# Four of the twelve token-weight tiles turned by DMA transposes instead of TensorE, with the first half of the step list rearranged

## The chip, the cores and the metric

One core of one Trainium2 chip runs one kernel launch. The metric is device time in microseconds of that launch. The kernel before was run three times: 165.80 us is the median, 165.77 and 166.24 us are the ends. Its inputs and its output are in the chip's memory; five engines take part: TensorE (PE; its weight loads are listed apart, as PEld), VectorE (DVE), ScalarE (ACT), GpSimd (POOL) and SyncE (SP), which only issues transfers. ACT also issues transfers from its own queue, and POOL some from a third.

## What is computed

A recurrent attention with a decay for each head feeds a block that mixes tokens and channels. Batch is 4, heads 8, tokens 768, head width 64, so the model width is 512.

```python
for t in range(S):
    state = gamma * state + outer(k[:, :, t], v[:, :, t])
    y[:, :, t] = scale * q[:, :, t] @ state
x = y with heads side by side                       # (4, 768, 512)
theta = x @ w_theta
zr, zi = x * cos(theta), x * sin(theta)
y = w_tok_r @ zr + w_tok_i @ zi                     # over tokens, for each batch
u = x + y
out = u + relu(u @ w_ch)
```

## The kernel before

The recurrence is computed in chunks. A unit `n` (0 to 23) is one batch, one chunk of 256 tokens and half of the heads: batch `n // 6`, chunk `n // 2 % 3`, half `n % 2`. A tile `C` or `t` (0 to 23) is 128 tokens of one batch, all 512 columns; units 0 and 1 make tiles 0 and 1, units 2 and 3 make tiles 2 and 3, and so on. The third number in a step such as `M.3.1` is a token tile of the same batch.

The order of all work is written out by hand as one list of steps, `ORDER`. Each step `name.args` calls the function of that name, which issues its instructions at once; a trailing letter picks the engine (`v` DVE, `a` ACT, `p` POOL) or, for loads and stores, the queue (`s` SP, `a` ACT). Each engine and each queue runs its own instructions strictly in the order of the list, and semaphores make an instruction wait for its data. So the list sets, for each engine, what stands behind a waiting instruction.

The steps, in the order in which a unit and then a tile go through them:

- `Lk`, `Lq`, `Lv` load 256 KB of k, q or v. The tiles are `kqf` (16 buffers for k and q together) and `vf` (9).
- `ck`, `cq` cast k and q to bf16; `cqs` (line 342) casts q and scales it by a decay in one pass; `cv` (line 348) scales v. Results are `kqb` and `vb`.
- `Tk`, `Tq` (line 356) turn k and q with four 128x128 transposes each on TensorE, into `kq_ps`; `E` copies that to `kqT`. `Dk` (line 372) does both with one DMA transpose on SP's queue.
- `A` (line 390) makes the scores in the one buffer `at_ps`; `m` (line 399) multiplies them by the causal mask on DVE; `I` (line 455) and `Y` (line 467) add what the state and the chunk give to the output; `ST` (line 417), `S0`, `S1`, `SB` carry the state on.
- `XB` copies the unit's output to `xT`, where q was scaled by `cqs`; `XA` (line 485, DVE only) copies and scales it, where q was only cast by `cq`.
- `Tx` (line 499) and `Ex` turn `xT` to `x_sb` by TensorE and a copy; `Dx` (line 506) does it with one DMA transpose on SP.
- `Hh` (line 513) makes theta; `CN` (line 520) takes sine and cosine on ACT; `z` (line 527) multiplies by x, on DVE or POOL.
- `Pw.r.g` loads a group of rows of token weight `r` (0 real, 1 imaginary) on POOL's queue, with a cast to bf16: group 0 is row tile 0, group 1 tiles 1 and 2, group 2 tiles 3 to 5. `Pth` and `Pch` load the two channel weights.
- `Tw.r.t` (line 535) turns row tile `t` of weight `r` with six 128x128 transposes on TensorE into `w_ps`, and `Ew` copies it to its place in `wtr` or `wti`.
- `M.t.s` (line 553) adds two matmuls, weights 0 and 1, of source tile `s` to the output tile `t`; it needs the turned weights of row tile `t % 6` and `z` of source tile `s`. The first batch's tile 3 needs `Tw.0.3` and `Tw.1.3`, its tile 5 needs `Tw.0.5` and `Tw.1.5`.
- `u`, then `Tu` and `Eu`, or `Du` (line 575) by a DMA transpose on SP, then `O` (line 580), `f` and the store `SO` finish a tile.
- `Z` runs two matmuls on zeros: filler for TensorE, with no result that is used.

The constants are steps too. `const3` computes two tables of decays with Exp on ACT (line 274), `const8` and `const9` the rest of them; `const7` runs Sin once on one number (line 285), `const6` zeroes the block-diagonal state tiles (line 306).

Of the kernel before, what the change touches and what calls it, by code (L numbers as in the profile page):

```python
# [677 lines left out]
```

## Time and profile before

| | before |
|---|---|
| median of three runs | 165.80 us |
| the profiled execution, its own time | 165.54 us |
| its span, first to last instruction | 163.8 us |
| TensorE clock granted over the span | 1.000 |
| DMA transposes issued by SP | 37 (16 `uT`, 12 `x_sb`, 9 `kqT`) |
| bytes read from memory, written to it | 25.69 MB, 6.29 MB |
| 16 DMA engines' share: SP's and ACT's queues, POOL's queue | 67.6% + 15.2%, 12.4% |

The profile is of one execution. Its span leaves 1.7 us of the measured time outside. A row of a group or timeline gives line, engine, operation, output <- inputs, shapes and a count; "idle before" is the time that the engine stood still ahead of these instructions, with the releaser that ended it. Rows of an engine's name with a q (SPq, ACTq) are issues on its queue. Matmul ends are modelled, so what one of a row of matmuls costs is best read from how far apart they start.

### The profile page before, as it was taken

Reading aid. Unit: us, or ns where it says so; the run is one execution under the profiler, and the core shown is the slowest. Engines: PE = TensorE matmul, PEld = TensorE weight load, DVE = VectorE, ACT = ScalarE, POOL = GpSimd, SP = SyncE. Lnnn points to the kernel's source line nnn. Section 1 sums busy time; section 2 is a strip of 40 time slices with the busy share of each in tenths; the row PEclk is TensorE's granted clock in tenths of the full one; section 3 lists DMA queues with packets and bytes.
Section 4 is the critical chain, followed back from the end, with each engine's and each line's share of the span. In section 5 each row is a group of like instructions: output and inputs, shape, how many; then the busy total and the mean of one; then the engine's idle time right before and its main releaser. Section 6 shows DMA issues by size and latency. Waiting matters only on the chain.

```text
span 163.8 us, 4900 instructions
## 1 busy us (share of the span) xinstructions
PE 153.7 (94%) x2001; PEld 87.1 (53%) x2030; DVE 115.2 (70%) x218; ACT 79.5 (49%) x142; POOL 77.3 (47%) x111
## 2 busy tenths in 40 slices
PE   5997889999999999999999999999999999999992
PEld 1355655756666655654555565554554544444550
DVE  5488687987994897994779894798867760244462
...
GB/s 130 318 317 255 279 310 233 268 230 214 207 193 202 308 220 198 309 135 259 341 270 198 192 229 189 223 151 292 218 267 116 96 92 202 160 70 123 71 243 203
DMA packets 62918, 34.93 MB, mean 213 GB/s; under 512 B 26416, under 2 KB 59952, under 8 KB 62896
## 3 DMA queue, kind: packets, MB, share of 16 engines
q1 hardware_dynamic: 51680, 23.73, 67.6%
q10 hardware_dynamic: 8528, 7.47, 15.2%
q0 software_dynamic: 2688, 3.41, 12.4%
q8 instruction: 16, 0.26, 0.7%
...
HBM read 25.69 MB, written 6.29 MB: 195 GB/s over the span
## 4 chain that ended last, share of the span: by engine, by line
PE 84%; DVE 5%; POOL 4%; issue 3%; ACT 1%; DVEq 0%; POOLq 0%
PE y_ps L553 36%; PE o_ps L580 12%; PE th_ps L513 12%; PE r_ps L467 5%; PE at_ps L390 4%; PE kq_ps L356 3%; PE r_ps L455 3%; PE w_ps L535 3%; DVE at L399 2%; PE x_ps L499 2%; PE y_ps L605 2%; PE r_ps L417 2%; PE u_ps L565 1%; DVE kqT L140 1%; POOL mask L298 1%
## 5 line engine op out<-in xcount | busy, mean ns | idle before, releaser
L553 PE MATMUL y_ps<-z,wti 128*128 128x512 bf16 x131 | 49.6, 379 | 1.0 <-issue 1.0
L553 PE MATMUL y_ps<-z,wtr 128*128 128x512 bf16 x131 | 49.7, 379 | 0.3
L527 POOL TENSOR_TENSOR z<-cs,x_sb 128x1024 bf16<-128x1024 bf16 x12 | 25.3, 2122 | 17.4 <-DMA x_sb<-xT 9.8
L399 DVE TENSOR_TENSOR at<-at_ps,mask 128x1024 bf16<-128x1024 f32 x24 | 29.2, 1216 | 0.6 <-PE at_ps L390 0.5
L348 POOL TENSOR_TENSOR vb<-vf,vsc 128x512 bf16<-128x512 f32 x17 | 18.2, 1071 | 21.3 <-DMA vf<-in_v_dram 20.3
L586 DVE SCALAR_TENSOR_TENSOR ot<-o_ps,u 128x512 f32<-128x512 f32 x23 | 15.8, 688 | 12.8 <-PE o_ps L580 12.7
L513 PE MATMUL th_ps<-wth,xT 128*128 128x512 bf16 x88 | 23.9, 379 | 0.5
L560 DVE TENSOR_TENSOR u<-y_ps,x_sb 128x512 bf16<-128x512 f32 x23 | 15.8, 688 | 11.9 <-PE y_ps L553 11.8
L580 PE MATMUL o_ps<-wch,uT 128*128 128x512 bf16 x88 | 23.2, 379 | 0.4 <-issue 0.2
L520 ACT ACTIVATE cs<-th_ps,zerob 128x512 bf16<-128x512 f32 x24 | 16.4, 685 | 12.6 <-PE th_ps L513 8.1
L520 ACT ACTIVATE cs<-th_ps,halfpi 128x512 bf16<-128x512 f32 x24 | 16.3, 684 | 10.8 <-issue 4.6
L140 POOL CAST sbd<-s 64x256 bf16<-64x256 f32 (+1 forms) x21 | 10.0, 478 | 22.9 <-DVE s L435 21.7
L553 PEld LDWEIGHTS <-wtr 128*128 128x128 bf16 x138 | 13.5, 98 | 12.7
L553 PEld LDWEIGHTS <-wti 128*128 128x128 bf16 x138 | 13.5, 98 | 11.9 <-DVE wti L140 0.2
L138 ACT COPY kqT<-kq_ps 128x1024 bf16<-128x1024 bf16 x12 | 12.1, 1012 | 10.4 <-PE kq_ps L356 10.4
L138 ACT CAST kqb<-kqf 128x512 bf16<-128x512 f32 x17 | 10.2, 619 | 6.8 <-DMA kqf<-in_k_dram 6.7
L513 PEld LDWEIGHTS <-xT 128*128 128x128 bf16 x96 | 8.8, 98 | 8.2
L580 PEld LDWEIGHTS <-uT 128*128 128x128 bf16 x92 | 8.4, 98 | 8.6
L356 PE MATMUL kq_ps<-ident,kqb 128*128 128x128 bf16 x120 | 11.2, 219 | 0.5 <-ACT kqb L138 0.2
L311 PE MATMUL zz<-zero 128*128 128x512 bf16 x27 | 9.7, 494 | 2.0 <-DVE part L232 1.9
L467 PE MATMUL r_ps<-at,vb 64*64 64x128 bf16 x384 | 9.9, 221 | 1.0 <-DVE at L399 1.0
L356 PEld LDWEIGHTS <-kqb 128*128 128x128 bf16 x120 | 8.1, 98 | 4.7 <-ACT kqb L138 0.7
...
## 6 DMA issues: line engine op xcount, KB each, us to landing
vf<-in_v_dram SPq DMA_DIRECT2D x20, 256.0 KB, 5.7
kqf<-in_k_dram SPq DMA_DIRECT2D x19, 256.0 KB, 5.0
kqf<-in_q_dram SPq DMA_DIRECT2D x17, 256.0 KB, 5.3
out_dram<-ot ACTq DMA_DIRECT2D x12, 256.0 KB, 2.8
out_dram<-ot SPq DMA_DIRECT2D x11, 256.0 KB, 3.1
kqf<-in_q_dram ACTq DMA_DIRECT2D x7, 256.0 KB, 5.3
kqf<-in_k_dram ACTq DMA_DIRECT2D x5, 256.0 KB, 5.2
vf<-in_v_dram ACTq DMA_DIRECT2D x4, 256.0 KB, 5.3
```

The lines of the kernel that those rows point to most:

```text
L138: nc.scalar.copy(dst, src)
L348: engines[e].tensor_mul(in_blocks(vb), by_token(raw["vf", n]), _bcast_last(K["vsc"][:, i, :, h * HU:(h + 1) * HU], D))
L356: nc.tensor.transpose(st["kq_ps", n][:, 4 * w + x, :], st["kqb", n][:, w, x * P:(x + 1) * P], K["ident"])
L399: nc.vector.tensor_mul(at.rearrange("p g j a t -> p (g j) (a t)"), st["at_ps", n].rearrange("p g j a t -> p (g j) (a t)"), _bcast_mid(K["m ...
L467: nc.tensor.matmul(st["R", n + 1][c][g * D:(g + 1) * D, j * P:(j + 1) * P], st["vb", n][rows, lo:lo + D], st["at", n][rows, g, j, a, :], s ...
L513: nc.tensor.matmul(th_ps, st["xT", C][:, j, :], K["wth"][:, j, :], start=(j == 0), stop=(j == 3))
L520: nc.scalar.activation(st["cs", C][:, w, :], st["th_ps", C], AF.Sin, bias=K["zerob" if w else "halfpi"], scale=1.0)
L527: engines[e].tensor_mul(st["z", b][:, c], st["cs", C], _bcast_mid(x_of(C), 2))
L553: nc.tensor.matmul(st["y", t], K["wT"][r][:, s0, t0 * P:(t0 + 1) * P], st["z", b][:, s0, r, :], start=(done == 0 and r == 0), stop=(done = ...
L560: nc.vector.tensor_add(st["u", t], st["y", t], st["x", b][:, t0, :])
L580: nc.tensor.matmul(o_ps, st["uT", t][:, j, :], K["wch"][:, j, :], start=(j == 0), stop=(j == nD - 1))
L586: nc.vector.scalar_tensor_tensor(st["ot", t], st["o", t], 0.0, st["u", t], ALU.max, ALU.add)
```

## The change

`Dw` is new: one DMA transpose on SP's queue takes a bf16 row tile (128x768) to its place in `wtr` or `wti`. Row tiles 3 and 5 of both weights go that way; their four `Tw` and four `Ew` are gone. Unit 15's k and q go by `Dk` instead of `Tk`, `Tq` and `E`; tile 5's u by `Du` instead of `Tu` and `Eu`; tiles 8 and 12 go from `Tx` and `Ex` to `Dx`, tile 13 the other way. In all, TensorE issues 40 transposes fewer: 24 of weights, 8 for unit 15, 4 for tile 5's u and 4 for x.

`const3` is split: the Exp of `vsc` stays in it, that of `qsc` is the new step `constS`. `const7`, the Sin on one number, moves ahead of both. Loads move between SP and ACT; several casts and copies change engine; which units scale q early (`cqs`, then `XB`) and which late (`cq`, then `XA`) changes. The last 296 of the steps are the same.

```diff
ORDER = """
-const2 Lv.0.s const1 constQ const6.v Z.29 Z.2 const5 Z.38 Lk.0.a const3 Z.35 Z.8 Lq.0.s Lv.1.s Z.28 constA
-const4 Lq.1.a cqs.0.v const9 Lk.1.s cv.0.p Z.39 const8 ck.0.p Tk.0 Tq.0 ck.1.a E.0.v Lq.4.a ST.0
-Lk.4.a Z.15 A.0 cqs.1.p Tq.1 Lq.2.s S0.0.v SB.0.1.v Lk.2.s SB.0.0.p cv.1.p Lv.2.s S1.0 I.0 Z.27 m.0
-Tk.1 E.1.a Y.0 ST.1 XB.0.1.a cqs.2.v Z.34 S0.1.v S1.1 cv.2.p SB.1.0.a Pth Lq.3.s Z.18 XB.0.0.v Tq.2
-A.1 SB.1.1.a ck.2.a Tk.2 const7 I.1 Z.23 m.1 Y.1 XB.1.0.a Lk.3.s E.2.v XB.1.1.v A.2 ck.3.p m.2 ST.2
-S0.2.v S1.2 SB.2.1.a Z.11 cqs.3.p Tq.3 Lv.3.s Tx.0 Tk.3 Z.3 ck.4.p Lv.4.s Lk.5.s Lq.5.s Lv.5.s
-Lq.6.s Lk.6.s Lv.6.s Lq.7.s E.3.a SB.2.0.v I.2 Y.2 XB.2.1.a Ex.0.a cv.3.v cq.4.p Tk.4 Lq.8.s A.3
-ST.3 Lk.7.s S0.3.v SB.3.0.a S1.3 Lv.7.s Lk.8.s Tx.1 Tq.4 SB.3.1.p cv.4.p m.3 Pw.1.0 XB.2.0.a Ex.1.a
-I.3 Lv.8.s E.4.a cq.5.a Y.3 Pw.0.0 ST.4 Hh.0 ck.5.a S0.4.v XB.3.0.v XB.3.1.v cv.5.v CN.0.1 A.4
-CN.0.0 Tq.5 Hh.1 Tk.5 SB.4.0.p SB.4.1.a Pw.0.1 Hh.2 m.4 E.5.v I.4 Y.4 ST.5 ck.6.a Tk.6 Tx.2 cq.6.a
-CN.1.1 CN.1.0 XA.4.1 A.5 XA.4.0 m.5 Lq.9.s Ex.2.v S0.5.v z.0.p Tq.6 E.6.a CN.2.0 cv.6.p Hh.3
-SB.5.0.v Tx.3 Tw.1.0 z.1.v SB.5.1.a Ew.1.0.v Ex.3.a CN.2.1 A.6 I.5 Y.5 ST.6 XA.5.0 z.2.v Tw.0.0
-CN.3.0 Tx.4 CN.3.1 Ew.0.0.v S0.6.v XA.5.1 Ex.4.v Hh.4 CN.4.0 CN.4.1 Tw.0.1 M.0.1 Pw.1.1 z.3.v M.0.0
-Tw.0.2 Pw.1.2 Ew.0.2.a SB.6.1.a Hh.5 z.4.p SB.6.0.p Lk.9.a M.0.3 ck.7.p cqs.7.p M.0.2 CN.5.1 CN.5.0
-cq.8.a m.6 Ew.0.1.v Tw.1.1 Tw.1.2 Ew.1.1.v Lv.9.s M.0.4 M.1.0 Tx.5 Ew.1.2.v M.1.1 S1.6 Tk.7 M.1.4
-Pch Ex.5.v z.5.v cv.7.v Tq.8 Tq.7 M.1.2 E.7.a M.0.5 I.6 Y.6 ST.7 A.7 ck.8.a u.0 S0.7.v m.7 XA.6.1
-SB.7.1.a M.1.5 M.1.3 XA.6.0 Tw.1.3 M.2.5 Pw.0.2 M.2.3 u.1 S1.7 Tk.8 M.2.1 M.2.0 SB.7.0.v Ew.1.3.a
-Tu.0 I.7 cv.8.p E.8.a cv.9.p Y.7 ST.8 A.8 cqs.9.v ck.9.v M.2.4 Du.1 Lk.10.s Eu.0.a XB.7.1.a XB.7.0.v
-S0.8.v SB.8.0.v M.2.2 Tx.6 Tq.9 Tk.9 Lv.10.a cv.10.p ck.10.p Lq.10.s S1.8 u.2 m.8 O.0 E.9.a SB.8.1.a
-Hh.6 Tw.1.4 I.8 Y.8 A.9 CN.6.0 Du.2 Lq.14.s CN.6.1 Ex.6.v f.0 ST.9 Tw.0.3 Hh.7 Ew.1.4.v Ew.0.3.a
-S0.9.v Tw.0.4 M.3.0 Tw.1.5 CN.7.0 CN.7.1 M.3.2 Dx.7 M.3.1 M.3.5 M.3.3 Lv.12.s Lk.12.s Ew.1.5.v
-XA.8.1 Ew.0.4.v Lq.12.s M.3.4 u.3 S1.9 Tw.0.5 Tk.10 M.4.5 cqs.10.p XA.8.0 m.9 M.4.3 Tq.10 SB.9.1.a
-SB.9.0.a I.9 O.2 Lq.11.s Lk.11.s E.10.a Lk.15.s Ew.0.5.v Lk.14.s Y.9 ST.10 A.10 z.7.p Lv.11.s
-XB.9.1.a XB.9.0.a f.2 M.4.0 O.1 M.4.1 cqs.14.p m.10 S0.10.v f.1 cq.11.a ck.12.v M.4.4 M.4.2 Tu.3
-Eu.3.a Dx.9 SB.10.0.a cqs.12.p u.4 Hh.9 Tq.11 ck.11.v Tu.4 z.6.v Eu.4.v ck.15.v M.5.0 M.5.4 Tk.11
...
+const2 Lv.0.s const1 constQ Z.8 const7 Lq.0.s Lk.0.s constA const3 Z.2 Z.35 Z.11 const4 Lv.1.a constS Z.38
+Z.27 Lk.3.s const5 cqs.0.v cv.0.v ck.0.v Lq.1.s Tk.0 Lk.2.a Tq.0 const9 ck.3.v cqs.1.v ST.0 Tq.1 Z.28 Z.29
+S0.0.v E.0.v Lk.1.s A.0 Lq.4.a ck.1.p cv.1.p const8 const6.v Tk.3 Lq.2.a SB.0.1.a Lv.2.s SB.0.0.a Tk.1 S1.0
+m.0 I.0 Pth Lv.3.s Z.39 Lk.4.s Y.0 E.1.a ck.2.v cq.2.p ST.1 Z.15 A.1 S0.1.v Tq.2 SB.1.1.a Tk.2 cv.3.p Z.3
+Lq.3.s cv.2.p cq.3.p SB.1.0.a XB.0.0.v cq.4.p XB.0.1.v S1.1 m.1 I.1 E.2.a Lv.4.s Y.1 ST.2 A.2 S0.2.v
+SB.2.1.p XB.1.0.v Z.34 S1.2 Tq.3 SB.2.0.a XB.1.1.a m.2 Lq.5.s Z.23 Lk.6.a Tx.0 Ex.0.v cv.4.p Lk.5.s I.2 Y.2
+Lv.5.s ST.3 E.3.a S0.3.v ck.4.a cqs.5.p A.3 Tk.4 SB.3.0.a XA.2.1 Lv.7.a Pw.1.0 Tq.4 Pw.0.0 Pw.0.1 SB.3.1.v
+Z.18 XA.2.0 E.4.a Hh.0 ck.5.a S1.3 I.3 Lq.6.s CN.0.1 Tx.1 m.3 Y.3 ST.4 A.4 XA.3.0 Pw.1.1 Ex.1.a CN.0.0 Tk.5
+Tq.5 E.5.a Lv.6.s S0.4.v Tx.2 m.4 SB.4.0.a Hh.1 CN.1.0 Lv.8.s cv.5.p XA.3.1 A.5 CN.1.1 SB.4.1.p I.4 cqs.6.p
+Y.4 ST.5 z.0.v S0.5.v ck.6.v Ex.2.a Hh.2 Tk.6 XA.4.1 SB.5.0.p Tq.6 CN.2.0 z.1.v XA.4.0 Hh.3 E.6.a SB.5.1.p
+m.5 Lq.8.a I.5 cv.6.p Tw.1.0 Ew.1.0.v Tx.3 Y.5 ST.6 CN.2.1 A.6 Ex.3.v XB.5.0.v CN.3.1 Tw.0.0 z.2.p Hh.4
+Lq.7.s Ew.0.0.v Lk.8.s Tx.4 XB.5.1.a Tw.0.1 CN.3.0 S0.6.v Ex.4.v CN.4.0 S1.6 M.0.2 Ew.0.1.v Pw.1.2 Tx.5
+M.0.0 Lk.7.s CN.4.1 Pw.0.2 Tw.0.2 Hh.5 SB.6.1.v z.3.v Ew.0.2.a cv.7.v z.4.v Lq.9.s CN.5.1 M.0.1 ck.7.p
+SB.6.0.p Tw.1.1 M.0.3 CN.5.0 Ew.1.1.v M.0.4 M.1.3 M.1.4 Ex.5.a cv.8.v z.5.v M.1.0 M.1.2 cq.7.a Tk.7 Tq.7
+Lk.9.s m.6 Tw.1.2 Lv.9.s M.0.5 M.1.1 Dw.1.3 E.7.v I.6 cqs.9.v Y.6 u.0 ST.7 A.7 ck.8.a Ew.1.2.a Tk.8 XB.6.1.v
+S0.7.v SB.7.0.v M.2.5 m.7 SB.7.1.v cqs.8.p Tq.8 XB.6.0.a M.2.4 S1.7 Tu.0 M.2.2 M.2.1 E.8.v Pch I.7 Eu.0.v
+M.1.5 cv.9.p Y.7 ST.8 S0.8.v XA.7.1 ck.9.a Lq.11.s A.8 Dw.0.3 Tk.9 Tw.1.4 XA.7.0 u.1 Lq.10.s Ew.1.4.a Du.1
+M.2.3 S1.8 Tq.9 SB.8.1.p M.2.0 SB.8.0.a Hh.6 Dw.0.5 u.2 I.8 m.8 Tx.6 O.0 E.9.a CN.6.1 Lk.10.a CN.6.0 Y.8
+ST.9 S0.9.v f.0 cqs.10.p A.9 Tw.0.4 Du.2 SB.9.0.a XB.8.1.v Hh.7 Ex.6.a cqs.11.p M.3.1 Ew.0.4.a Lv.10.a
+Lk.11.a M.3.3 SB.9.1.p M.3.2 M.3.0 M.3.4 CN.7.0 M.3.5 m.9 cv.10.p Tq.10 Dx.7 Dw.1.5 CN.7.1 M.4.0 Lq.12.a
+ck.10.v M.4.1 M.4.4 u.3 M.4.2 XB.8.0.v Lk.14.s z.6.v S1.9 z.7.p O.2 Tk.10 ck.11.p Lv.11.s M.4.3 M.4.5 I.9
+Lk.12.s f.2 O.1 E.10.a cv.11.p Lq.15.a u.4 Y.9 ST.10 f.1 A.10 Tq.11 XB.9.1.a M.5.1 M.5.5 M.5.2 Lv.12.a Tk.11
+S0.10.v m.10 M.5.4 Lq.14.s SB.10.1.p Hh.9 Tu.3 ck.12.p ck.14.a E.11.v cqs.12.p SO.2.s M.5.3 Dx.9 Lq.13.a
...
@@ -267,12 +262,14 @@
     def const3():
         K["qsc"] = const.tile([P, 2, nI * 4, 2], FT, name="qsc")
         K["vsc"] = const.tile([P, nI, 2, H], FT, name="vsc")
-        for t, arg, bias, sc in (
-                (K["qsc"].rearrange("p h x g -> p (h x) g"),
-                 K["argq"].rearrange("p h x g -> p (h x) g"), K["lscale"], 1.0),
-                (K["vsc"].rearrange("p i a h -> p (i a) h"), K["arg"], K["zerob"], -1.0)):
-            nc.scalar.activation(t, arg, AF.Exp, bias=bias, scale=sc)
+        nc.scalar.activation(K["vsc"].rearrange("p i a h -> p (i a) h"), K["arg"], AF.Exp,
+                             bias=K["zerob"], scale=-1.0)
         K["qx"] = const.tile([P, H // 2, S], FT, name="qx")
+
+    def constS():
+        nc.scalar.activation(K["qsc"].rearrange("p h x g -> p (h x) g"),
+                             K["argq"].rearrange("p h x g -> p (h x) g"), AF.Exp,
+                             bias=K["lscale"], scale=1.0)
 
     def const8():
         decay(0, 2 * P)
@@ -534,6 +531,11 @@
         for s0 in range(nT):
             nc.tensor.transpose(w_ps[:, s0, :], row[:, s0 * P:(s0 + 1) * P], K["ident"])
         st["w_ps", r, t0] = w_ps
+
+    def Dw(r, t0):
+        g = sum(t0 >= hi for _, hi in groups)
+        nc.sync.dma_start_transpose(out=K["wT"][r][:, :, t0 * P:(t0 + 1) * P],
+                                    in_=K["row"][r][g][:, t0 - groups[g][0]])
 
     def Ew(r, t0, e):
         copy(e, K["wT"][r][:, :, t0 * P:(t0 + 1) * P], st["w_ps", r, t0])
```

73 lines of the change are left out of this document (35 added, 38 removed).

## The prediction

> **What bounds the kernel now.** I read the page's head first, then the sums by stage (busy us of each engine, the granted clock, the DMA share, GB/s), then the chain of waits and the timelines of the first 56 us.
>
> ```profile
> span 163.8 us, 4900 instructions
> PE 153.7 (94%) x2001; PEld 87.1 (53%) x2030; DVE 115.2 (70%) x218; ACT 79.5 (49%) x142; POOL 77.3 (47%) x111
> 0.00:8.00 8.00, 6.00 (x19) 2.22 (x20) 4.18 (x15) 4.63 (x8) 6.33 (x36) 1.00 0.76 221
> 8.00:16.00 8.00, 6.91 (x164) 4.40 (x164) 6.70 (x13) 6.84 (x14) 7.17 (x9) 1.00 1.15 291
> 16.00:24.00 8.00, 6.58 (x141) 4.57 (x142) 5.84 (x13) 6.42 (x12) 3.78 (x7) 1.00 1.14 293
> 24.00:32.00 8.00, 7.65 (x153) 5.13 (x153) 6.71 (x14) 7.33 (x13) 4.59 (x4) 1.00 1.14 254
> 64.00:72.00 8.00, 7.81 (x144) 4.88 (x144) 6.75 (x13) 5.28 (x10) 4.44 (x4) 1.00 0.91 262
> 152.00:164.00 12.00, 8.55 (x52) 4.58 (x51) 5.20 (x9) 1.33 (x3) 0.00 (x0) 1.00 0.60 174
> ```
>
> TensorE is busy 153.7 of 163.8 us, so it stands still 10.1 us. The first four stages hold 32 - 27.14 = 4.9 us of that (and the zero matmuls as filler), the last one about 3.3 us of its span. That leaves under 2 us for the 120 us between: from the fourth stage to the tail TensorE sets the time, and what is taken off its queue there comes off the end, as long as nothing it needs gets later. In the first 32 us chains of other engines set it.
>
> **The 40 transposes taken away.**
>
> ```profile
> 33.46 0.34 PE w_ps L535 x6
> 35.52 0.67 PE w_ps L535 x12
> 38.37 0.45 PE kq_ps L356 x8
> ```
>
> These are pieces of the chain of waits. Twelve transposes follow each other in 0.67 us, eight in 0.45: 0.056 us each. The diff takes away 24 + 8 + 4 + 4 = 40: **-2.24 us**, all at places after 41 us where TensorE is the bound. The copies that fall away with them (Ew, E, Eu, Ex) free DVE and ACT, which are at 70% and 49%; I give nothing for that.
>
> **The start.** The rearranged steps make some things later, and I follow unit 0 and then unit 5.
>
> ```profile
> 2.73 0.51 SPq L164 DMA_DIRECT2D kqf<-in_k_dram  x1
> 4.90 0.61 SPq L160 DMA_DIRECT2D kqf<-in_q_dram  x1
> SPq L160 <- DMA kqf<-in_k_dram: 1.6, 1, 1.6
> kqf<-in_q_dram SPq DMA_DIRECT2D x17, 256.0 KB, 5.3
> 3.28 1.09 DVE L306 MEMSET sbd<- 128x256 uint32 x4
> 8.40 0.69 DVE L140 COPY kqT<-kq_ps 128x1024 bf16<-128x1024 bf16 x1 [1.18 <-PE kq_ps L356]
> 9.88 1.21 DVE L399 TENSOR_TENSOR at<-at_ps,mask 128x1024 bf16<-128x1024 f32 x1
> 11.02 0.68 DVE L342 TENSOR_TENSOR kqb<-kqf,qsc 128x512 bf16<-128x512 f32 x1
> ```
>
> In the list before, the fifth load on SP (Lq.2, at 4.90) waited 1.6 us until a k load had landed that ACT had issued. It is the ninth of both queues together, and no data ties it to that load: I read a ring of eight completion slots that SP's and ACT's transfers share in the order of the list. In the new list Lq.1 is SP's fifth but the sixth of both, so it need not wait: it goes out some 0.6 us after the fourth at 2.73, near 3.3, and lands 5.3 us later at about 8.6. DVE now has E.0 behind ck.3 and cqs.1: cqs.1 (0.68) ends near 9.3, E.0 (0.69) near 10.0, then const6 (1.09), which has moved here, and S1.0 (0.28, an estimate from such adds); m.0 starts near 11.3 where it started at 9.88. Unit 0 is 1.4 us late.
>
> ```profile
> 27.20 1.22 DVE L399 TENSOR_TENSOR at<-at_ps,mask 128x1024 bf16<-128x1024 f32 x1
> 29.30 0.35 PE at_ps L390 x16
> 29.92 0.42 PE L467 MATMUL r_ps<-at,vb 64*64 64x128 bf16 x16
> 12.80 0.62 ACT L138 CAST kqb<-kqf 128x512 bf16<-128x512 f32 x1
> 13.44 1.28 ACT L285 ACT_TABLE_LOAD   x1
> 14.73 0.29 ACT L285 ACTIVATE one<-zerob,halfpi 128x1 f32<-128x1 f32 x1
> ```
>
> Before, m.5 ended at 28.42 and Y.5 began at 29.92: 1.5 us of slack, since TensorE had other work queued ahead. That absorbs the 1.4. But const7 was what loaded ACT's Sin table at 13.44, in a gap. In the new list it runs first, Exp (const3, constS, const9, const8) puts another table in its place, and the first CN has to load Sin again: a third load, 1.28 us, between ck.5 and CN.0.1, with E.5 three steps behind it. A.5 waits for E.5, and in the new list I.4 and Y.4 stand behind A.5 on TensorE. So Y.5 is between on time (the load falls into ACT's slack) and 1.4 + 1.28 - 1.5 = 1.2 us late. Besides, A.6 (0.35) stood ahead of Y.5 and now stands behind it, so an equal Y.5 is a loss of 0.35. Cost of the start: 0.35 to 1.55; a gain is not excluded for units 2 to 4, whose loads come earlier, and I let the bottom end be -0.5. I take **+0.5**, near the end where the slack covers, since ACT is 6.42 of 8 us busy there and has 20% to give.
>
> [...]
>
> **The four DMA transposes, on SP's queue.**
>
> ```profile
> 27.37 1.52 POOL L187 DMA_DIRECT2D row<-in_moe_w_tok_i_dram  x2
> row<-in_moe_w_tok_i_dram POOLq DMA_DIRECT2D x1, 576.0 KB, 11.9
> row<-in_moe_w_tok_r_dram POOLq DMA_DIRECT2D x1, 576.0 KB, 8.9
> 30.89 0.69 DVE L527 TENSOR_TENSOR z<-cs,x_sb 128x1024 bf16<-128x1024 bf16 x1
> L527 POOL TENSOR_TENSOR z<-cs,x_sb 128x1024 bf16<-128x1024 bf16 x12 | 25.3, 2122 | 17.4 <-DMA x_sb<-xT 9.8
> L372 SPq DMA_TRANSPOSE kqT<-kqb x9: 1231/1252/2490, 60.0 to 122.3; - x9
> uT<-u SPq DMA_TRANSPOSE x16, 3.4
> kqT<-kqb SPq DMA_TRANSPOSE x9, 4.6
> 45.46 0.63 SPq L160 DMA_DIRECT2D kqf<-in_q_dram  x1
> 50.94 1.04 POOL L342 TENSOR_TENSOR kqb<-kqf,qsc 128x512 bf16<-128x512 f32 x1
> 55.23 0.39 PE L356 MATMUL kq_ps<-ident,kqb 128*128 128x128 bf16 x4
> 51.82 2.16 PE y_ps L553 x10
> ```
>
> No transpose of a weight by DMA is in this trace; a Dw moves 192 KB, between a Du (128 KB, lands in 3.4 us) and a Dk (256 KB, 4.6), and keeps SP 1.2 to 2.5 us, as the Dks do. I take 1.25 and a landing after 4.0.
>
> What comes late is the rows. Pw.1.2, the second of the pair at 27.37, now stands on POOL behind z.2, which DVE ran at 30.89 and POOL now runs in 2.12 us from about 29.7 (an estimate: CN.2 ends a little earlier in the new list). It goes out near 31.8 and lands 11.9 later, near 44; Pw.0.2 right behind it lands 8.9 to 11.9 after 32.6, near 44 too. So SP sits at Dw.1.3 until 44, then issues Dw.1.3 (to 45.3), Lq.11 (to 45.9), Dw.0.3 (to 47.2) and Lq.10 at 47.2 where it stood at 45.46. Behind these wait Du.1, Dw.0.5, Du.2, Dx.7, Dw.1.5 and the loads of units 11 to 14.
>
> Two things are due. M.3 (the row of 51.82 is M.3 and what follows) now begins with M.3.1: three Tw and two M (3 x 0.34 + 2 x 0.43) are no longer ahead of it, so it is due near 50.0 + 0.5; Dw.0.3 lands at 47.2 + 4 = 51.2. And Tq.10, which started near 55.0 in the row of 55.23, is due near 55.0 - 4 x 0.34 - 0.22 - 2 x 0.43 + 0.5 = 53.1 (four Tw, Tk.10 and two M fewer ahead); Lq.10 lands at 47.2 + 5.3 = 52.5, cqs.10 takes 1.04, ready at 53.5. TensorE stands 0.7 us for the first, and the second is then covered by it. The ends: 0, if the rows land 8.9 us after their issue as the real weight's did, and 4 us, if each Dw keeps SP 2.5 us and lands after 5.5. I take **+0.7**, with the median issue of nine Dks rather than the longest.
>
> ```profile
> q1 hardware_dynamic: 1633, 0.39, 38.8%
> x_sb<-xT SPq DMA_TRANSPOSE x2, 2.4
> DMA  9999999996299999999999006999999999999999
> ```
>
> **The DMA engines.** The first two rows are of the stretch from 127 to 132 us, where three 128 KB transposes (0.39 MB) are nearly all that moves: 38.8% of 5 us is 1.94, 0.65 us of all 16 engines each. The change adds four of 192 KB, one of 256 KB and two of 128 KB (Dx 12 and 8 for 13 make one, Du.5 the other): 4 x 0.97 + 1.3 + 1.3 = 6.5 us of all engines, four fifths of it between 44 and 80 us. The third row is DMA in 40 slices from 42 to 60 us: full, but for three slices of 0.45 us. From 64 to 72 us the share is 0.91 where the stages from 8 to 24 us reach 1.15 (records overlap, so a share can pass 1): 0.24 x 8 = 1.9 us of room, and 1.3 in the idle slices. These 3.2 us hide half of it; the other half I cost at nothing as well, on the guess that the loads that it delays are not the next ones due. With that cover gone it is 3.3 us.
>
> **Sum.** -2.24 + 0.5 + 0.7 = -1.0 us on the profiled execution's 165.54 (span 163.8 and 1.74 around it). The median of the runs is 0.26 above that; I carry the difference over: 165.8 - 1.0 = **164.8 us**. Less than 0.3% (0.5 us) is about what a measurement of this kernel can't tell from no change.
>
> **Rivals.**
>
> *All of it hidden.* Rows land early, the table load falls into a gap. For it: 1.5 us of slack at Y.5, ACT and POOL under 50% on the whole. Against: the 0.35 at A.6, the row loads behind z.2. 165.8 - 2.24 + 0.2 = 163.8. Chance 0.13.
>
> *The start eats it.* Unit 0's 1.4 us and the table load add up at A.5: 1.55, and the 0.7 stays: 165.8 - 2.24 + 2.25 = 165.8, no change. For it: DVE is 6.7 of 8 us busy in two of the four stages, so a lag is not soon made up. Chance 0.17. [...]
>
> *SP's queue is held (slower).* A transpose waits on SP for rows that a third queue brings; everything behind it waits as well, and by the ring of eight so does ACT's Lv.10, the eighth transfer after Dw.1.3. Tq.10 then waits for Lq.10's issue + 5.3 + 1.04 - 53.1. The change breaks even where that is 2.24 - 0.5 = 1.74, with Lq.10 issued at 48.5, and is slower from there. With the Dws at 2.5 us each and the rows 1 us later, Lq.10 goes at 50.7, and the wait is 3.9: 165.8 - 1.74 + 3.9 = 168.0. For it: Lq.10's margin before, 55.0 - 52.0 = 3 us, is used up in my sum. Against: the long issue is one of nine. Chance 0.22.
>
> *The DMA engines become the bound (slower).* 6.5 us more of them in stretches with few idle slices delay v loads, which POOL already waits for; the uncovered 3.3 us on the path give 164.8 + 3.3 = 168.1. Chance 0.12.
>
> [...] Then it is far over 168; 0.02.
>
> **How the numbers follow.** The forecast itself has 0.34, with its own range 164.1 to 165.4. Faster by over 0.3%: 0.34 x 0.94 + 0.13 + 0.02 from the other cases' edges = 0.47. Slower: 0.22 + 0.12 + 0.02 + a quarter of the start's case, 0.40. Between: 0.13. The range for 8 in 10 goes from 163.5 (all hidden, the start 0.3 better than that) to 168.0.
>
> **What would show it.** Right: 72 - 24 = 48 `w_ps` matmuls; three table loads, the last just ahead of the first CN on ACT; first mask multiply near 11.3; SP's first weight transpose near 44 and a TensorE wait under 1 us at M.3 or Tq.10; idle time of TensorE between 32 and 152 us still under 3 us. Wrong: Y.5 later than 31.2; SP issuing Lq.10 after 48.5; new rows in the table of waits in which TensorE waits for wtr, wti, kqb or vb for more than 1 us; v loads landing over 7 us after issue between 44 and 80 us.

## The result, and the profile after

The changed kernel takes 175.18 us in the median of its first four runs and 173.81 us in the median of four more; the kernel before took 165.96 and 166.2 us beside them. The ratio is 1.045 (95% interval 1.042 to 1.048) and, the second time, 1.046 (1.041 to 1.051): 7.6 us slower. Forecast were 164.8 us and a range up to 168.0; both the sign and the range were wrong. The executions fall into two groups, near 173.4 and near 177 us: the ratios compare the faster ones, and the profile below is of that group (173.09 us).

The head of the page of the changed kernel, then its sums by stretch (the stretch, its length, busy us of TensorE, its weight loads, VectorE, ScalarE and GpSimd with counts, granted clock, DMA share, GB/s):

```profile
span 171.1 us, 4847 instructions
PE 150.9 (88%) x1961; PEld 83.8 (49%) x1990; DVE 114.1 (67%) x211; ACT 74.3 (43%) x133; POOL 80.7 (47%) x121
0.00:8.00 8.00, 4.79 (x20) 1.93 (x20) 3.40 (x14) 6.48 (x10) 4.26 (x34) 1.00 0.76 207
8.00:16.00 8.00, 5.37 (x115) 3.42 (x115) 6.43 (x16) 4.52 (x10) 4.67 (x6) 1.00 1.14 314
16.00:24.00 8.00, 6.17 (x181) 4.58 (x182) 5.34 (x12) 5.90 (x9) 7.55 (x11) 1.00 1.18 275
24.00:32.00 8.00, 6.18 (x110) 3.91 (x102) 5.78 (x11) 6.72 (x12) 3.81 (x5) 1.00 1.14 238
32.00:50.00 18.00, 15.54 (x254) 9.82 (x258) 16.92 (x31) 8.24 (x15) 7.75 (x10) 1.00 1.13 223
85.00:115.00 30.00, 26.44 (x403) 14.67 (x409) 21.38 (x39) 13.56 (x27) 19.95 (x23) 1.00 1.05 226
32.00:152.00 120.00, 112.69 (x1467) 61.68 (x1488) 84.22 (x146) 49.38 (x93) 60.36 (x67) 1.00 1.01 209
```

The last three stretches in the kernel before:

```profile
32.00:50.00 18.00, 17.63 (x277) 11.56 (x280) 15.34 (x33) 11.53 (x20) 8.11 (x9) 1.00 1.17 216
85.00:115.00 30.00, 29.28 (x429) 16.23 (x425) 24.86 (x47) 13.64 (x26) 20.54 (x22) 1.00 1.13 207
32.00:152.00 120.00, 117.98 (x1482) 66.25 (x1503) 86.59 (x158) 52.90 (x96) 55.38 (x56) 1.00 0.97 203
```

TensorE's work did fall: 2.8 us less busy in all. But it stands still 9.5 us in the first 32 (4.9 before) and 7.3 us from 32 to 152 (2.0 before). Of the second, 2.1 us more lie between 32 and 50 us and 2.8 more between 85 and 115. So 9.9 us of new idle time stand against some 2.2 us of transposes saved: 7.7, where the spans differ by 7.3. The table of waits of the changed kernel names what TensorE stood for (engine, output and line, what ended the wait: us in all, times, longest):

```profile
PE y_ps L554 <- DVE z L523: 2.4, 2, 2.1
PE kq_ps L352 <- DVE kqb L338: 1.9, 1, 1.9
PE kq_ps L352 <- DVE kqb L134: 1.3, 1, 1.3
PE r_ps L413 <- DVE vb L344: 1.1, 1, 1.1
PE at_ps L386 <- DMA kqT<-kqb: 1.0, 2, 0.6
```

The first of these is in the middle, the next two are the start's (a line that waits 1.9 us for `part` is in both kernels and is left out), the last two have their longest waits near 89 and 99 us. Before, the table has no wait of TensorE for a transfer. None here is for `wtr` or `wti`, the tiles that the new transposes fill. `after` is this changed kernel, and in the expectations below "lost time" at a step is its start less what the steps ahead of it take on TensorE at full clock, zero matmuls not counted.

### The profile page after: what moved, and what is told of

Its sections match the earlier page's. It is cut to its first block, busy times and chain, and to the rows that moved or that the text cites. A ratio compares the mean times of both kernels' runs of the same rounds, so it can differ in the third digit from the quotient of the medians.

```text
span 175.5 us, 4847 instructions
## 1 busy us (share of the span) xinstructions
PE 153.2 (87%) x1961; PEld 84.6 (48%) x1990; DVE 114.7 (65%) x211; ACT 74.3 (42%) x133; POOL 81.8 (47%) x121
## 4 chain that ended last, share of the span: by engine, by line
PE 59%; DMA 16%; DVE 13%; SPq 3%; issue 3%; ACT 2%; ACTq 0%; DVEq 0%
PE y_ps L555 25%; PE o_ps L582 11%; PE th_ps L510 7%; DMA vf<-in_v_dram 4%; DVE at L396 4%; DMA kqf<-in_q_dram 4%; PE r_ps L464 4%; DMA uT<-u 3%; DMA kqT<-kqb 3%; PE at_ps L387 3%; DVE z L524 2%; DMA kqf<-in_k_dram 2%; PE kq_ps L353 2%; DVE vb L345 2%; PE r_ps L452 2%
## 5 line engine op out<-in xcount | busy, mean ns | idle before, releaser
L555 PE MATMUL y_ps<-z,wtr 128*128 128x512 bf16 x135 | 52.2, 387 | 3.1 <-DVE z L524 2.5
L555 PE MATMUL y_ps<-z,wti 128*128 128x512 bf16 x126 | 48.7, 386 | 0.4 <-issue 0.3
L135 POOL CAST sbd<-s 64x256 bf16<-64x256 f32 (+1 forms) x26 | 12.0, 462 | 37.0 <-DVE s L432 34.8
L524 POOL TENSOR_TENSOR z<-cs,x_sb 128x1024 bf16<-128x1024 bf16 x10 | 21.1, 2124 | 11.6 <-ACT cs L517 10.7
L339 POOL TENSOR_TENSOR kqb<-kqf,qsc 128x512 bf16<-128x512 f32 x13 | 13.4, 1040 | 5.9 <-DMA kqf<-in_q_dram 5.8
L353 PE MATMUL kq_ps<-ident,kqb 128*128 128x128 bf16 x112 | 10.2, 227 | 4.1 <-DVE kqb L339 2.2
L135 POOL CAST kqb<-kqf 128x512 bf16<-128x512 f32 x13 | 7.9, 625 | 9.6 <-DMA kqf<-in_k_dram 7.7
L133 ACT CAST kqb<-kqf 128x512 bf16<-128x512 f32 x13 | 7.9, 623 | 10.6 <-DMA kqf<-in_k_dram 10.5
L524 DVE TENSOR_TENSOR z<-cs,x_sb 128x1024 bf16<-128x1024 bf16 x14 | 11.2, 799 | 1.2 <-DMA x_sb<-xT 1.1
L133 ACT COPY kqT<-kq_ps 128x1024 bf16<-128x1024 bf16 x9 | 9.1, 1012 | 6.4 <-PE kq_ps L353 6.3
```

The lines of the kernel that those rows point to most:

```text
L133: nc.scalar.copy(dst, src)
L135: engines[e].tensor_copy(dst, src)
L353: nc.tensor.transpose(st["kq_ps", n][:, 4 * w + x, :], st["kqb", n][:, w, x * P:(x + 1) * P], K["ident"])
L524: engines[e].tensor_mul(st["z", b][:, c], st["cs", C], _bcast_mid(x_of(C), 2))
L555: nc.tensor.matmul(st["y", t], K["wT"][r][:, s0, t0 * P:(t0 + 1) * P], st["z", b][:, s0, r, :], start=(done == 0 and r == 0), stop=(done = ...
```

## The experiments

All ratios are to the kernel before, on the same chip in the same rounds; 1% is 1.66 us.

### The four DMA transposes, alone

**e1_dw_alone** keeps before's list and puts the four `Dw` in (it has the two Exp of the constants in the new order, as have the runs built on it).

```diff
-Tw.1.3 M.2.5 Pw.0.2 ... Ew.1.3.a ... Tw.0.3 Ew.0.3.a ... Tw.1.5 Ew.1.5.v ... Tw.0.5 Ew.0.5.v
+Pw.0.2 Pch ... Dw.1.3 Du.1 Lk.10.s ... Lq.10.s Dw.0.3 ... Du.2 Dw.0.5 Dw.1.5 Lq.14.s
```

> The order and the engines of before; of the change only the four sets of six transposes of tiles 3 and 5 (24 matmuls) and their four copies are replaced by the four DMA transposes, issued on SP at the steps where the copies stood or a little earlier (the pooled constant Pw.0.2 moves ahead of Pch). Theory A (the four DMA transposes are harmless; the loss comes from the other order of the first half): 24 x 0.056 = 1.3 us less TensorE work if the ring of completions holds nothing, so 164.3 to 166.0, no wait of TensorE above 0.5 us at M.3 or at the steps that read wtr. Rival B (SP's queue is held by the transposes and the loads behind them come late): 167 to 169, with idle time of TensorE ahead of Tq.10, Tk.12 or O.2.

Measured: 171.24 us, ratio 1.036 (1.032 to 1.040), 5.9 us slower than before. Theory A falls, and rival B's 167 to 169 was too low as well. SP's timeline in e1 (start, duration, what is issued):

```profile
45.86 1.87 SPq L536 DMA_TRANSPOSE wtr<-row  x1
47.82 2.91 SPq L576 DMA_TRANSPOSE uT<-u  x1
50.79 1.37 SPq L536 DMA_TRANSPOSE wtr<-row  x1
52.21 2.11 SPq L536 DMA_TRANSPOSE wti<-row  x1
54.42 0.61 SPq L154 DMA_DIRECT2D kqf<-in_q_dram  x1
```

and in the kernel before:

```profile
46.51 1.21 SPq L575 DMA_TRANSPOSE uT<-u  x1
47.81 0.61 SPq L160 DMA_DIRECT2D kqf<-in_q_dram  x1
```

The same load, Lq.14, is issued at 54.42 and not at 47.81, since four transposes and a slower one of u stand ahead of it; all loads behind it move with it. Of the first `Dw` (39.6 us) nothing is waited for. The second, at 45.86, is late (groups of weight loads between 45 and 60 us, then one row of the table of waits, both of e1):

```profile
L554 PEld LDWEIGHTS <-wtr 128*128 128x128 bf16 x9 | 0.9, 97 | 2.0 <-DMA wtr<-row 1.2
PE o_ps L581 <- DMA wch<-in_moe_w_ch_dram: 1.3, 1, 1.3
```

TensorE waits 1.2 us at M.3.0 for it, 1.3 us for `wch`, whose load now stands behind Pw.0.2 in GpSimd's queue, and later for the casts of late loads.

**g0_no_turn** has e1's list, but nothing is turned for tiles 3 and 5.

```diff
     def Dw(r, t0):
-        nc.sync.dma_start_transpose(...)
+        pass
...
+            w0 = t0 - (t0 in (3, 5))
-... K["wT"][r][:, s0, t0 * P:(t0 + 1) * P]
+... K["wT"][r][:, s0, w0 * P:(w0 + 1) * P]
```

> As e1_dw_alone (171.2 us), but the token weights of tiles 3 and 5 are not turned at all, neither by DMA nor on TensorE: the products of those tiles read the turned columns of tiles 2 and 4. So the 24 matmuls and four copies are gone at no price. If the DMA transposes' price is the whole loss of e1: 165.5 - 1.3 = 164.2 (163.5 to 165). If what else e1 moved (Pw.0.2 ahead of Pch, the missing copies) costs by itself: 166 to 171.

Measured: ratio 1.001 (0.998 to 1.004). The 24 matmuls are gone, and nothing is won: the rows that the new transposes need early (Pw.0.2) went ahead of `wch`, and TensorE waits 0.9 us for that. e1 less g0 is what the four transposes cost at these places of this list, the waits for their results included: 1.0356 - 1.001 = 3.5%, **5.7 us**.

**i2_one_block** and **i3_plain_copy** ask which property of them costs this.

```diff
+        w2 = work.tile([P, P], BF, name="w2", bufs=4)
+        nc.sync.dma_start_transpose(out=w2, in_=K["row"][r][g][:, t0 - groups[g][0], :P])
```

> As g0_no_turn (166.3 us: tiles 3 and 5 not turned, their products read tiles 2 and 4), with four DMA transposes at the places of e1, each of only one block of 128x128 and not six, into a tile that nobody reads. Theory F (the price is the time of the 16 DMA engines, some 5 us for 24 blocks): a sixth of e1's loss, 166.3 + 0.8 = 167.1 (166.3 to 168). Rival B (SP's queue is held and the ring of completions turns, whatever the size): 170 to 172 as e1.

```diff
-        nc.sync.dma_start_transpose(out=K["wT"][r][:, :, t0 * P:(t0 + 1) * P],
-                                    in_=K["row"][r][g][:, t0 - groups[g][0]])
+        nc.sync.dma_start(out=K["wT"][r][:, :, t0 * P:(t0 + 1) * P],
+                          in_=K["row"][r][g][...].rearrange("p (s t) -> p s t", s=nT))
```

> As e1_dw_alone (171.2 us), with four plain copies of the same 128x768 weights into the same places in pieces of 128 numbers (256 bytes), so untransposed, in place of the four DMA transposes; all waits of e1 stay. If the price is in the bytes and the 256-byte pieces: 170 to 172. If it is in the transposing (its engine time, or the 1.4 to 2.1 us for which one holds SP): 166 to 168. M.3.0's wait for wtr (1.2 us) tells how long one takes to land.

Measured: i2 1.015 (1.008 to 1.022), i3 1.010 (1.004 to 1.016), both nearer to g0 than to e1 (i3's five runs go from 166.27 to 170.93 us). Four small transposes hold SP 1.2 us each, as their rows in i2's timeline of SP show, and are as many transfers as e1's:

```profile
39.51 1.19 SPq L537 DMA_TRANSPOSE w<-row  x1
46.38 1.20 SPq L537 DMA_TRANSPOSE w<-row  x1
48.94 2.50 SPq L537 DMA_TRANSPOSE w<-row  x2
```

That is 4.9 us of SP against 6.7 in e1, and 2.3 us of price against 5.7 (in its trace the wait for `wch` alone is 2.2): the number of issues doesn't seem to make the most of it, though i2's interval leaves 1 to 3.5 us to it, and nobody waits for i2's results. The same bytes in 256-byte pieces, not transposed, cost 1.5 us, and there M.3.0 waits 1.3 us for `wtr`, as long as in e1, so that wait is not what makes e1 dear. The price goes with how much is transposed; but it goes with the time for which SP is held as well, 2.8 us in i3, 4.9 in i2 and 6.7 in e1 for 1.5, 2.3 and 5.7. Whether it is the DMA engines' time or SP's hold is not separated.

**g1_dw_on_act** issues them from ScalarE.

```diff
-        nc.sync.dma_start_transpose(out=K["wT"][r][:, :, t0 * P:(t0 + 1) * P],
+        nc.scalar.dma_start_transpose(out=K["wT"][r][:, :, t0 * P:(t0 + 1) * P],
```

> As e1_dw_alone, with the four DMA transposes issued on ScalarE's queue, not on SP's. Rival B (SP's queue is held: 1.4 to 2.1 us each, 6.9 us in all, and the loads behind come late): SP is free, 165 to 168. Theory F (the 16 DMA engines are busy throughout to 120 us, and the four transposes give them about 4.6 us more each, 160.5 against 155.9 us of packets by the shares of the queues): as e1, 170 to 172.5, whoever issues them.

Measured: 1.093 (1.085 to 1.101), worse than either theory says. ScalarE computes as well, and it stands still 6.3 us ahead of its first copy behind the first `Dw` (ScalarE's timeline in g1; the bracket is idle time and what ended it):

```profile
49.30 1.32 ACTq L536 DMA_TRANSPOSE wti<-row  x1
50.67 0.59 ACT L132 COPY uT<-u_ps 128x512 bf16<-128x512 bf16 x1 [6.34 <-issue]
```

What the `Dw` waited for is not its row, which e1 had for the same step at 39.6 us. SP's timeline and table of waits in g1 show it:

```profile
43.84 1.29 SPq L576 DMA_TRANSPOSE uT<-u  x1
54.69 1.22 SPq L576 DMA_TRANSPOSE uT<-u  x1
SPq L576 <- DMA wtr<-row: 8.1, 1, 8.1
```

SP's transpose of 43.84 landed 5.4 us later, at 49.24, and ScalarE's went out at 49.30; ScalarE's next, of 51.37, landed 3.3 us later, at 54.67, and SP's went out at 54.69. The transposes of the two queues took turns here, each behind the landing of the other queue's. So g1 is not a test of the theories. On ScalarE, which computes as well, the wait stood in front of its other work, the 6.34 us ahead of that copy.

**j4_dw_pw_back** puts Pw.0.2 back.

```diff
-Pw.0.2 Pch ... M.2.5
+Pch ... M.2.5 Pw.0.2
```

> As e1_dw_alone (171.2 us), with the load Pw.0.2 back at its place of before, behind Pch. In e1, g0, i2 and i3 the weights wch, behind Pw.0.2 in GpSimd's queue, come 0.9 to 2.2 us late at O.0; here they should not, but the weights of Dw.0.3 land later. If the lateness of wch is a part of e1's loss by itself: 171.2 - 1.3 = 169.9 (169 to 170.7). If the row's lateness takes its place (SP waits at Dw.0.3 for it, M.3.0 later): 171 to 172.5.

Measured: four runs from 168.07 to 172.57 us, median 171.2. The wait for `wch` is gone from its trace, and 1.5 us for `wtr` stand there: the row's lateness took its place, as the second line said. The spread leaves the time itself open.

**e2_after_no_dw** is the converse in after's list.

```diff
-... Dw.1.3 ... Dw.0.3 ... Dw.0.5 ... Dw.1.5
+... Tw.1.3 Ew.1.3.a M.2.3 ... Tw.0.3 Ew.0.3.v Tw.0.4 ... Tw.1.5 Ew.1.5.v M.4.1 ... Tw.0.5 Ew.0.5.v O.2
```

> The order and the engines of after; the four DMA transposes are replaced by the four sets of six transposes on TensorE and their copies, as before had them. Theory A (the DMA transposes are harmless in after): TensorE gets its 1.3 us back on its path, 173.4 + 1.3 = 174.7 (173.5 to 176). Rival B (the DMA transposes hold SP's queue and delay the loads whose lateness the trace of after shows at 88 to 113 us): about 5.6 us less waiting than in after plus 1.3 us more work, 168 to 171.

Measured: 1.079 (1.072 to 1.085), slower than after. Its trace has new waits just where I put the steps back (0.9 and 0.7 us ahead of turned weights, at 50.0 and 55.5 us), so it says little about the transposes, and what the four `Dw` cost in after's own order is not measured. What it does say: without them the wait at ST.14 is still there, 2.9 us against 1.1. The tail's loss isn't theirs alone.

### The order of the first half

**e5_start_of_before** and **e3_head_of_before** take before's list up to a step and after's from there.

```diff
-const2 Lv.0.s const1 constQ Z.8 const7 Lq.0.s ... A.5 CN.1.1 SB.4.1.p I.4 cqs.6.p Y.4
+const2 Lv.0.s const1 constQ const6.v Z.29 Z.2 ... Hh.2 m.4 E.5.v I.4 Y.4
```

> The list of before through step Y.4 (28 us in before), then after's own list. If the start's 4.2 us are a loss by themselves and the stretch of 36 to 48 us keeps its own: 173.4 - 4.2 = 169.2 (168 to 170.5), and the VectorE copies z.3, cv.7 and z.4 are again over 1 us long. If the stretch of 36 to 48 us is only a consequence of the late start: 165 to 166, those copies 0.6 to 0.7 us. If neither matters: 173.

> The list of before through step Y.6 (in after that is at 48 us), then after's own list for all that is left, the four DMA transposes among it where their place is behind that step. TensorE's lost time against its useful work grew in after by 4.2 us up to Y.4, by 4.0 us from 36 to 48 us and by 5.6 us from 88 to 113 us. If the three are separate: the first two go, 173.4 - 8.2 = 165.2 (164 to 167). If the loss of the first 48 us is made good later anyhow (what stands after 88 us sets the end): 172 to 174. If everything late follows from the first part: 161 to 163.

Measured: e5 1.028 (1.023 to 1.033), against after's 1.046: **putting the start back wins 3.0 us** (its four runs go from 169.76 to 175.20 us). In its trace cv.7 is 1.51 us long too, so that doesn't need the late start; but z.4 takes 0.68 us and not 1.90, and TensorE waits 1.0 us at M.0.4 and not 2.1, so a part of the 3.0 may lie in the middle. e3 1.051 (1.047 to 1.056): the head up to 48 us put back brings nothing. The parts are not separate: in e3, with before's list ahead of Y.6, TensorE stands 0.8 us at Tq.10 and 3.3 us between ST.14 and A.17. What e3 lost was not followed further.

How the start goes in the changed kernel (VectorE, then TensorE, then ScalarE):

```profile
9.57 0.69 DVE L338 TENSOR_TENSOR kqb<-kqf,qsc 128x512 bf16<-128x512 f32 x1 [1.23 <-DMA kqf<-in_q_dram]
12.22 1.21 DVE L395 TENSOR_TENSOR at<-at_ps,mask 128x1024 bf16<-128x1024 f32 x1
10.32 0.40 PE L352 MATMUL kq_ps<-ident,kqb 128*128 128x128 bf16 x4 [1.94 <-DVE kqb L338]
22.87 1.28 ACT L516 ACT_TABLE_LOAD   x1
```

cqs.1 waits for Lq.1 until 9.57 (the prediction had it landed at 8.6), and E.0 and unit 0's scores stand behind it; m.0 starts at 12.22 and not at 11.3. The third table load is where it was foretold, and the activation behind it starts at 24.16, 0.01 us after the load.

**f1_unit0_first** tries to mend this in after itself.

```diff
-Z.8 const7 Lq.0.s ... Tq.0 const9 ck.3.v cqs.1.v ST.0 Tq.1 Z.28 Z.29 S0.0.v E.0.v Lk.1.s A.0 ... S1.0 m.0 I.0 Pth
+Z.8 Lq.0.s ... Tq.0 const9 E.0.v ST.0 S0.0.v A.0 m.0 ck.3.v cqs.1.v Tq.1 Z.28 Z.29 Lk.1.s ... S1.0 I.0 Pth const7
```

> After, with one edit at the start: E.0, S0.0, A.0 and m.0 stand ahead of ck.3, cqs.1 and Tq.1 on VectorE and TensorE, and const7 (the table of sines) goes back from the front to behind Pth. In after, cqs.1 waits for Lq.1 until 10.2 us and A.0 comes at 11.5 to 12.6 us (9.1 in before). Theory C (the start costs 3.0 us by itself): lost time at Y.4 from 18.1 to about 15.5 us, 173.4 - 2.7 = 170.7 (169.8 to 171.5). Rival (the list behind is limited by its loads and takes the gain back): 172.8 to 174.

Measured: 1.069 (1.063 to 1.075), 3.8 us slower than after. m.0 came at 9.80, but it pushed cqs.1 to 11.74, beside a GpSimd operation, where it took 1.52 us; Tq.1 stood until 13.3. A miss: unit 0 was not the one that the rest waited for.

### VectorE beside GpSimd

**f2_no_port**

```diff
-cqs.9.v ... ck.8.a ... cqs.8.p ... cv.9.p ... XB.8.1.v ... XB.8.0.v ... SB.13.1.v
+cqs.9.v cv.9.v ... ck.8.a cq.8.a ... XA.8.1 ... XA.8.0 ... SB.13.1.a
```

> After, with three small operations on other engines: unit 8's query cast on ScalarE (cq.8.a, scaled later in XA.8, not cqs.8.p), cv.9 on VectorE behind cqs.9 (not on GpSimd), SB.13.1 on ScalarE (not VectorE). In after, the VectorE operations cv.7 (1.53 us), z.4 (1.90 us) and SB.13.1 (1.30 us) run beside those GpSimd operations and end about 0.55 us after GpSimd's own. Theory P (VectorE's operations on SBUF stand still while GpSimd's run): cv.7 and z.4 fall to 0.68 us each, SB.13.1 to 0.4 us, TensorE's waits at M.0.4 and I.13 (2.1 and 1.3 us) go: 173.4 - 3.2 = 170.2 (169.3 to 171.3). Rival (the durations stay over 1 us whatever GpSimd does, or the loads take the gain back): 172.8 to 174.

VectorE (two rows, then one at 85 us) and GpSimd in after:

```profile
37.22 1.53 DVE L344 TENSOR_TENSOR vb<-vf,vsc 128x512 bf16<-128x512 f32 x1
38.67 1.90 DVE L523 TENSOR_TENSOR z<-cs,x_sb 128x1024 bf16<-128x1024 bf16 x1
85.00 1.30 DVE L134 CAST sbd<-s 64x128 bf16<-64x128 f32 x1
37.12 1.08 POOL L338 TENSOR_TENSOR kqb<-kqf,qsc 128x512 bf16<-128x512 f32 x1 [0.39 <-DMA kqf<-in_q_dram]
38.96 1.05 POOL L344 TENSOR_TENSOR vb<-vf,vsc 128x512 bf16<-128x512 f32 x1
85.18 1.04 POOL L338 TENSOR_TENSOR kqb<-kqf,qsc 128x512 bf16<-128x512 f32 x1
```

cv.7 ends at 38.75, 0.55 us behind GpSimd's 38.20; z.4 ends at 40.57, 0.56 behind 40.01. SB.13.1, a smaller operation, ends at 86.30, 0.08 behind GpSimd's 86.22, and not 0.55. In f2, z.3 and then the same two, and what GpSimd ran beside z.3:

```profile
36.92 1.11 DVE L523 TENSOR_TENSOR z<-cs,x_sb 128x1024 bf16<-128x1024 bf16 x1
37.96 0.77 DVE L344 TENSOR_TENSOR vb<-vf,vsc 128x512 bf16<-128x512 f32 x1
38.65 0.68 DVE L523 TENSOR_TENSOR z<-cs,x_sb 128x1024 bf16<-128x1024 bf16 x1
36.85 0.62 POOL L134 CAST kqb<-kqf 128x512 bf16<-128x512 f32 x1
```

Theory P holds for the durations: with GpSimd's two multiplies gone from beside them, 1.53 + 1.90 us became 0.77 + 0.68, and z.3, which now ran beside a cast on GpSimd, took 1.11 us where it had taken 0.69, ending 0.56 us behind that cast. For the time it is open: 1.047 (1.043 to 1.051) is after's own ratio. In f2's trace TensorE loses 3.2 us less than in after from 27 us on, but 1.9 us more in the start, where its granted clock was 0.75 from 8 to 12 us and 0.50 from 12 to 16. And the 3.2 us hoped for were read from one trace: TensorE waits 2.1 us at M.0.4 in it, but 0.9 us in h1's and 0.6 in j3's (the next section), which issue the same steps up to there.

### The tail's loads

**h1_loads_before_du1**, **j3_tail** and **j2_port_tail** (the edits of f2 and j3 together):

```diff
h1
-Lq.10.s Ew.1.4.a Du.1 ... Lk.10.a ... Lv.10.a Lk.11.a ... Lq.12.a ... Lk.14.s ... Lv.11.s
+Lq.10.s Lk.10.s Lv.10.s Lk.11.s Lq.12.s Lk.14.s Lv.11.s Ew.1.4.a Du.1
j3
-Lk.18.a ... Lk.15.s ... Lq.17.s m.14 Dk.15 ... ST.13 Lv.14.a
+Lk.15.a ... Lk.18.s ... Lq.17.s Lv.14.s m.14 Dk.15 ... ST.13
```

> After, with the loads Lk.10, Lv.10, Lk.11, Lq.12, Lk.14 and Lv.11 issued on SP right behind Lq.10, ahead of Du.1, and not in their places behind it (four of them on ScalarE's queue). In after SP waits 8.7 us for u.1 at Du.1, from 46 to 54 us, and the DMA engines' share falls to 0.54 from 50 to 60 us (1.24 in before). Theory D (that hole is what makes the loads of 88 to 113 us late): the hole goes (share above 0.9), what landed by 110 us rises by about 1 MB, the waits at ST.14, A.16 and O.10 shrink from 5.6 to under 2 us: 168 to 171. Rival E (those waits come from the order of the loads in the tail, Dk.15 ahead of Lv.14 and Lk.15 late, not from the hole): 172.5 to 174.

> After, with two edits in the list of loads: Lk.15 and Lk.18 change places (Lk.15 is asked for at 71 us and not at 78), and Lv.14 goes ahead of Dk.15 on SP (80 us, not 83 us on ScalarE's queue). In after's second execution Dk.15 is issued at 82.6 us, waits for casts of a unit whose keys land at 81.9, and Lv.14 lands at 89.8: ST.14 and A.15 lose 1.15 us (2.6 to 3.0 in others), A.16 0.7 us. Theory E (the order of these loads makes the tail late): those go, 173.4 - 1.9 = 171.5 (170.5 to 172.5). Rival F (the DMA engines are busy anyway, another transfer comes late in its place): 173 to 174.5.

> After, with the edits of f2_no_port and of j3_tail together. If the waits on GpSimd's operations (3.2 us in the trace of f2) and those of the tail (1.9 us) are separate: 173.4 - 5.1 = 168.3 (167.5 to 170), where TensorE's clock keeps full in the first 16 us. Where it falls there, as in the traces of f2 and h1: 170 to 172. If the loads take it back: 173.

Measured: h1 1.060 (1.054 to 1.065): theory D falls. The DMA engines' share from 50 to 60 us is 1.16 (0.54 and 0.90 in the profiles of two executions of after), and the waits of the tail stayed (1.4 us at ST.14, 1.1 at A.16), with 1.1 us at O.2 new, where Du.2 now stands behind the loads. j3 1.046 (1.039 to 1.052): the 1.1 us at ST.14 went and 0.5 came at A.15, the wait at A.16 grew from 0.6 to 1.4, and 0.9 came at a theta product at 108.8 us; rival F. j2 1.038 (1.032 to 1.043), 1.4 us under after and with intervals that touch, less than a third of the 5.1 hoped for.

### All parts together

**j1_start_port_tail** is e5 with the edits of f2 and j3; **k1_cv9_later** and **k2_ck16_earlier** mend what its traces showed.

```diff
k1
-cqs.9.v cv.9.v Y.6 u.0 ... E.8.v
+cqs.9.v Y.6 u.0 ... E.8.v cv.9.v
k2
-XB.13.1.a ... CN.13.1 ... ck.16.a
+XB.13.1.a ck.16.a ... CN.13.1
```

> The list of before through Y.4 as in e5_start_of_before (1.028 of before, about 170.3 us), then after's list with the edits of f2_no_port and of j3_tail. Theory C (start, GpSimd's port and the tail's loads are three separate losses): 170.3 - 1.0 (M.1.3) - 1.2 (I.13) - 2.0 (A.15) = 166.1 (165.3 to 167.5), within 1% of before, the DMA transposes still in it. Rival F (the DMA transposes' own price, 5 us in e1, stays in some other wait): 169.5 to 171.

> As j1_start_port_tail, with cv.9 moved behind E.8 on VectorE. In the trace of j1, cv.9 waits there for Lv.9, which lands at 43.1 us, and u.0 and the product M.2.5 wait behind it (3.1 us of TensorE). Theory C (start, port and tail are the losses): that wait goes, 170.0 - 3.1 = 166.9 (166 to 168). Rival F (the price of the DMA transposes shows up in another wait): 168.8 to 170.5, with new waits at M.3, O.2 or Tk.10 or behind.

> As k1_cv9_later, with the key cast ck.16 on ScalarE ahead of CN.13 and not behind it, so that SP can issue Dk.16 some 2.5 us earlier (92.0 us in j1, landing at 97.7, where A.16 loses 1.6 us). Theory C: a further 1.4 us off, 165.5 (165 to 167), the time of before or under it. Rival F: the same as k1 within 0.5 us, as the transfers behind come late in its place.

Measured: j1 from 169.47 to 179.35 us, median 173.28; its cv.9, moved to VectorE, waited there for Lv.9 and held u.0 and M.2.5 behind it, 3.2 us of TensorE by my own edit. k1 **1.015** (1.013 to 1.018), 2.5 us over before. k2 1.022 (1.018 to 1.026): slower than k1, the cast's gain went to new waits. So the start, VectorE's operations beside GpSimd's and the tail's loads, mended together, take away 5.1 of the 7.6 us; one by one only the start did. What is left in k1 are waits on transposes by DMA (the two largest in its table of waits that are not in before's):

```profile
PE at_ps L386 <- DMA kqT<-kqb: 1.7, 2, 1.5
PE o_ps L581 <- DMA uT<-u: 1.3, 2, 0.8
```

The 1.5 us stand at A.16, which waits for Dk.16. Here is its issue (with Dk.17 behind it) in k1, and then in the kernel before:

```profile
90.33 2.73 SPq L368 DMA_TRANSPOSE kqT<-kqb  x2
82.02 4.63 SPq L372 DMA_TRANSPOSE kqT<-kqb  x2
```

Before's list has Dk.16 ahead of Du.7 and its cast ck.16 fifty steps earlier; the new list has it behind Dx.12 and Du.7. So the order of the list is enough to explain that wait, and k2, which moved the cast alone, had Dk.16 issued only 0.35 us earlier. The longer of the other two, 0.8 us, is O.2's for Du.2, which stands behind three of the four `Dw`. How much of k1's 2.5 us is the price of the `Dw` is not shown: k1 was not run without them. It lies between what theory C and rival F said. No version ran faster than the kernel before.

## Why the prediction was wrong

**The four DMA transposes: the term was mis-sized.** The sum had -1.34 us (24 transposes), +0.7 for SP's queue and nothing for the DMA engines, "on the guess that the loads that it delays are not the next ones due". In before's order they cost 5.7 us (e1 less g0), because they were: in e1 TensorE waits 2.3 us for casts of late loads and 1.2 us for the weights themselves, in g0 0.2 us for the one and nothing for the other. The rivals had the right mechanisms: SP held, loads late, other transposes late; their 168.0 and 168.1 were each too low, and they were taken as alternatives where they may be one thing. The rows to go by were the DMA shares of 1.14 and more from 8 to 32 us, and the full slices from 42 to 60: with so little room there, work added to the DMA engines is to be priced as a loss until the opposite is shown. In after's own order, where the price is not known, M.3 and Tq.10 don't wait (M.3.1 at 55.1, later than the weights): that step came out as written, because all else was later. Each `Dw` kept SP 1.3 to 2.1 us there and landed after 5.5 to 6.8, not 1.25 and 4.0. The time did come out far over 168, the case given 0.02, but no run shows the size of the pieces to be the cause: in i3 the same bytes in 256-byte pieces, not transposed, cost 1.5 us.

**What is taken off TensorE comes off the end: only where nothing else is due.** g0 takes 24 matmuls away, its transposes cost nothing, and it gains nothing, for with one row load ahead of it `wch` was late by most of that. The 10.1 us of idle time showed that TensorE was the bound; they did not show how far behind it the next limit lay.

**The start: +0.5 was up to 3.0** (e5). Its mechanism was right, and the third table load with it. Lq.1 took 6.3 us to land and not the median's 5.3; Y.5 began at 32.14, past the 31.2 named as the sign of failure, so the 1.5 us of slack did not cover it. The ring of eight shared places was my reading of one wait, the 1.6 us at Lq.2, and no run shows it: in the new trace Lv.2, the eleventh transfer of both queues, goes out at 4.58 us, while Lk.0, the third, lands at 7.0. What Lq.2 waited for stays open.

**Two things were not in the sum.** The first is VectorE's operations that run beside GpSimd's (TensorE waits 2.1 us in the middle, 0.9 us at 87 us), though before's trace had the same case (cqs.0 took 1.47 us beside cv.0, others 0.68). The second is the tail: I followed SP's queue as far as Tq.10 and not to unit 14, where Lv.14 is asked for later and on another queue, and Dk.15 on SP waits for late keys, nor to Dk.16, which the new list asks for later. These prices are of different lists and can't be added up: with the 5.7 they come to more than the 7.6 us and the saving.

**What was right**: 48 transposes of weights, three table loads, the last ahead of the first CN, the first `Dw` at 41.0 us (44 said), Lq.10 at 45.2, no wait for `wtr` in after. These signs were true and did not matter. Two others did not come: the first mask multiply (12.22 and not 11.3) and an idle time under 3 us from 32 to 152 (7.3). Two of the signs of failure came true, Y.5's and the waits for `kqb` and `vb` over 1 us.
